# Seven groups of instructions change places in VectorE's queue, in batches 3 and 4

## The chip, the cores and the metric

The kernel runs on one core of a Trainium2 chip. The metric is the device time of one execution in microseconds. The kernel before took 396.45 us, the median of three runs (395.72 to 396.65).

## The reference

Two blocks follow each other. The first is an mLSTM cell over 4 batches, 8 heads, 768 steps and a head size of 40; the second is a Fourier mix with a two-layer perceptron on the 320 joined features.

```python
for t in range(S):                                    # mLSTM, per batch and head
    m_new = max(f[t] + m, i[t])
    C = exp(f[t] + m - m_new) * C + exp(i[t] - m_new) * outer(v[t], k[t])
    n = exp(f[t] + m - m_new) * n + exp(i[t] - m_new) * k[t]
    y[t] = sigmoid(o[t]) * (C @ q[t]) / max(abs(n @ q[t]), 1)
x = y as (batch, 768, 320)
u = x + real(fft(fft(x, axis=1), axis=2))             # Fourier mix
un = (u - mean(u)) / sqrt(var(u) + 1e-6)              # over the 320 features
out = u + maximum(un @ w_ch1, 0) @ w_ch2              # 320 -> 1280 -> 320
```

## The kernel before, in words

**Tiles and stages.** In the text the batches are 1 to 4; in the code b is 0 to 3. A batch has six chunks of 128 steps (c = 0 to 5). Of batches 2 to 4 each chunk goes through the mLSTM in halves of 64 steps; then the whole batch goes through the Fourier mix (two steps of matrix products), and then through the perceptron. The stages of neighbouring batches overlap: while the perceptron of one batch runs on TensorE, the mLSTM of the next runs in between, and after it the mix of the next.

**The steps that the change touches**, with the lines of the profile:

- `halves_weigh` (L672): VectorE multiplies a chunk's scores, in a bank of PSUM, by its weights W. `halves_from_chunk` (TensorE, L519) then multiplies W by the values.
- `mlstm_finish` (L712 to L720, five instructions): VectorE forms the denominator and multiplies the heads' result `ph`, in PSUM, by the gate. There is one bank pair for the heads: the next chunk's `halves_from_state` (TensorE, L519 `ph<-C,qg`) writes where `mlstm_finish` has read. The chunks 0, 1 and 3 are written into `so` and moved to their rows by DMAs (`halves_rows`, L728); chunks 2, 4 and 5 are written straight into `x`.
- `halves_add` (L667): VectorE adds a product from PSUM to the state C.
- `mix_add` (L957 to L963, six instructions): VectorE adds the result `pu` of the feature transform to `x` in four pieces and takes mean and variance. The chunks come in the order 0, 5, 1, 4, 2, 3; a pair shares one bank of `pu`. ScalarE's `mix_center` (L971) follows, then a transpose on TensorE (L978 `put`).
- `mlp_sums` (L1106, four instructions): the first layer is done by a scheme with seven products in place of eight, which needs sums of the inputs: T3, a new B12, T2 and T4, in this order.
- `mlp_block`: one pass of this scheme over two columns of hidden blocks, in four steps. VectorE adds products from PSUM (L1127) to the hidden values h; TensorE's products are L1118 and the short ones of the remaining 64 features L1123. A pass uses four banks; the next pass begins in the bank of the product p3, once VectorE has added it.
- `mlp_out_pair`: the second layer, also by seven products, two chunks at a time (three pairs n, four steps each). Two banks x and y alternate. After each product VectorE adds it, scaled, to the output (`residual`, L1187), which frees the bank for the next product (TensorE, L1237).
- `hidden_sums` (L1223): VectorE's sums for that scheme.

**What sets the order.** Nothing is scheduled by a compiler. `at(slot, phase, function, ...)` enters a call in a plan; at the end the plan is sorted by slot, then phase, and the calls issue their instructions in that order, each engine's queue being filled so. The phases are named EVAC 0, FILL 1, MAIN 2, FILL_PE 3. A step of the perceptron on TensorE is at MAIN of its slot, with the VectorE additions that belong to it. The perceptron of batch 2 fills the slots 63 to 94, that of batch 3 the slots 95 to 126, that of batch 4 those from 127 on. The mLSTM of batch 3 begins at slot 53 and its mix at slot 83; for batch 4 it is 83 and 115. Chunk c of a batch has its own slot s, three more for each c. An engine works its queue in this order and waits at a semaphore where an input is not there yet.

```python
            at(s + 1, FILL + 0.55 if b == 1 and c > 0 else MAIN + 0.7, halves_weigh, b, c)
            at(s + (5 if (b, c) == (2, 2) else 4), FILL + 0.3 if b == 1 else MAIN + 0.55, mlstm_finish, b, c)
            at(a, FILL if b < 2 else MAIN + 0.5, mix_add, b, c)
            at(s_mlp, EVAC + 0.5, mlp_sums)
```

Of the kernel before, what the change touches and what calls it, by code (L numbers as in the profile page):

```python
# [53 lines left out]
def kernel(  # L54
# [69 lines left out]
    def at(slot, phase, fn, *args):  # L124
        plan.setdefault((slot, phase), []).append((fn, args))
# [7 lines left out]
    EVAC, FILL, MAIN, FILL_PE = range(4)  # L133
# [628 lines left out]
    def plan_halves(b, s0, stride=3):  # L762
        for c in range(NT):
            s = s0 + stride * c
            t = 22 + 2 * c if b == 1 and c < 3 else s - 5
            at(t, FILL, mlstm_load, b, c)
            at(t, FILL, mlstm_load_max, b, c)
            at(34 if b == 1 and c == 2 else t + 1, FILL, mlstm_load_decay, b, c)
            at(s - 1, FILL, mlstm_load_o, b, c)
            at(s - 1, FILL, mlstm_scale_v, b, c)  # L770
            at(s - 1, FILL + 0.3, mlstm_exp, b, c, 0)
            at(s, FILL, mlstm_exp, b, c, NP)
            at(s, FILL_PE + 2.05, halves_scores, b, c)
            at(s, FILL_PE + 2.5, halves_to_state, b, c)
            for i in range(2):
                at(s + i, FILL + 0.05, halves_decay, b, c, i)
                at(s + 1 + i, FILL - 0.2, halves_add, b, c, i)
            at(s, FILL + 0.1, mlstm_scale_q, b, c)
            at(s + 1, FILL, mlstm_mask, b, c)
            at(s + 1, FILL + 0.55 if b == 1 and c > 0 else MAIN + 0.7, halves_weigh, b, c)  # L780
            end = c == NT - 1
            at(s + 3, MAIN - 0.1 if end else FILL_PE, halves_from_state, b, c)
            at(s + 3, MAIN - 0.1 if end else FILL_PE, halves_from_chunk, b, c, 0)
            at(s + 3, MAIN if end else FILL_PE + 0.5, halves_between, b, c)
            at(s + 3, FILL_PE + 3, halves_from_chunk, b, c, 1)
            at(s + 3, FILL_PE + 0.6, mlstm_tanh, b, c)
            at(s + (5 if (b, c) == (2, 2) else 4), FILL + 0.3 if b == 1 else MAIN + 0.55, mlstm_finish, b, c)
            at(s + 6, FILL - 0.6, halves_rows, b, c)


# [216 lines left out]
    def plan_mix(b, s0, x_done, s_feat, s_add, s_turn):  # L1007
        for j in range(TG):
            p = TG - 1 - j
            at(x_done[j] + (b > 1 and j == TG - 1), FILL + 0.5 if b < 2 else FILL_PE + 0.2, mix_fold, b, p)  # L1010
            if b == 0:
                at((s0 - 4, s0 - 2, s0)[j], FILL_PE + 4, mix_seq, b, p, (0, 1))
                at((s0 - 2, s0 - 2, s0)[j], FILL_PE + 4, mix_tail, b, p)
            elif b == 1 or j == 0:
                if b > 1:
                    for step, slot in enumerate((x_done[0], x_done[-1] + 2, x_done[-1] + 6)):
                        at(slot, FILL_PE + 0.25, mix_fold_again, b, step)
                at(s0, FILL_PE + 4, mix_seq, b, p, (0,))
                at(s0 + 1, FILL_PE + 4, mix_seq, b, p, (1,))
                at(s0 + 2, FILL_PE + 4, mix_tail, b, p)  # L1020
        for i in range(2):
            at(s0 + 1 if b == 0 else s0 + 1 + i, FILL, mix_seq_out, b, i)
        at(s0 + (1 if b == 0 else 3), FILL + 0.1, mix_tail_out, b)
        for p in range(TG):
            at(s_feat[p], FILL_PE + 4, mix_feat, b, p)
        for c, a, t in zip(ORDER, s_add, s_turn):
            at(a, FILL if b < 2 else MAIN + 0.5, mix_add, b, c)
            at(t, FILL + 0.1, mix_center, b, c)
            at(t, FILL_PE + (5 if b == 0 or c in ORDER[:4] else -0.1), mix_turn, b, c)
            if b > 0:  # L1030
                at(t, FILL_PE + 6, mix_turn_out, b, c)
            elif t < s_mlp:
                at(t + 1, FILL + 0.2, mix_turn_out, b, c)
            else:
                at(t + 1, EVAC, mix_turn_out, b, c)
# [62 lines left out]
    def mlp_u(gr, ch):  # L1098
        return uT_bufs[gr][:, ch].rearrange("p c t -> p (c t)")

    def mlp_sums():

        T2, T3, T4 = w1x["T"]
        B11, B12, B21, B22 = mlp_u(0, 0), mlp_u(1, 0), mlp_u(0, 2), mlp_u(1, 2)
        for out, x, y in ((T3, B22, B12), (B12, B12, B11), (T2, B22, B12), (T4, B21, T2)):
            nc.vector.tensor_tensor(out=out, in0=x, in1=y, op=OP.subtract)  # L1106

    def mlp_block(b, i, step):
# [200 lines left out]
    def plan_batch(b, s_mlstm, s_mix, s_mlp):  # L1309
        (plan_halves if b > 0 else plan_mlstm)(b, s_mlstm)  # L1310
        done = [s_mlstm + n for n in ((16, 19, 22) if b == 0 else (18, 21, 22))]
        assert s_mix >= done[-1] and s_mlp >= s_mix + 9
        late = [s_mlp + 2 * c for c in range(TG)]
        if b == 0:
            feat = [s_mix + 1, s_mix + 1, s_mlp + 3]
            turn = [s_mix + 2, s_mix + 3, s_mix + 4]
            add = turn + [s_mlp, s_mlp + 4, s_mlp + 5]
            late = [s_mlp + 2, s_mlp + 5, s_mlp + 7]
        else:
            feat = [s_mix + c for c in ((3, 4, 6) if b == 1 else (3, 4, 7))]  # L1320
            add = [s_mix + c for c in ((4, 4, 5, 6, 7, 7) if b == 1 else (4, 5, 5, 6, 8, 9))]
            turn = [s_mix + c for c in ((5, 6, 6) if b == 1 else (6, 7, 8))]
            late = [s_mix + c for c in ((7, 8, 8) if b == 1 else (9, 10, 10))]
            at(s_mlp, EVAC + 0.5, mlp_sums)
        plan_mix(b, s_mix, done, feat, add, turn + late)
        s = s_mlp + NFF + 2
        at(s, FILL + 0.6, mix_rstd, b)
        for n in range(3):
            at(s + 3 * n if b == 0 else s, FILL + 0.65, mix_rstd_step, b)
        plan_mlp(b, s_mlp)  # L1330

    s_mlp = 31
    plan_batch(0, 0, 22, s_mlp)
    plan_batch(1, 32, 54, s_mlp + MLP_SLOTS)
    plan_batch(2, 53, 83, s_mlp + 2 * MLP_SLOTS)
    plan_batch(3, 83, 115, s_mlp + 3 * MLP_SLOTS)
    for n in range(4):
# [149 lines left out]
```

## Time and profile before

| | us |
|---|---|
| median of three runs | 396.45 |
| the profiled execution | 395.51 |
| its span | 393.8 |
| TensorE busy (PE) | 378.9 (96%) |
| VectorE busy (DVE) | 277.9 (71%) |
| ScalarE busy (ACT) | 172.1 (44%) |
| GpSimd busy (POOL) | 134.3 (34%) |
| TensorE's granted clock over the span | 1.0 |

The span is the time from the first to the last instruction; 1.7 us of the execution lie outside it. A line of the timeline gives start, duration, engine, line, operation, the tile written and the tiles read, the shapes and a count where equal instructions were merged. Square brackets give the engine's idle time ahead of it and the instruction that ended the idle time. Consecutive VectorE instructions overlap by some 0.08 us, so a group's length is taken from start to start.

### The profile page before, as it was taken

The numbers are of one execution on the slowest core, as the hardware profiler recorded it, in microseconds if no ns is written. First come the engines' busy times: TensorE is split into PE (matmuls) and PEld (weight loads), VectorE is DVE, ScalarE is ACT, GpSimd is POOL, SyncE is SP. The second block draws the span as 40 slices with busy tenths as digits, with TensorE's granted clock in tenths as the row PEclk, the third lists the DMA queues.
The fourth block names the chain that finished last, engine by engine and source line by source line (L and its number), as shares of the span: only waits on it lengthen the run. The fifth ranks groups of instructions, "written<-read, shape, count | busy, mean of one in ns | idle before, by whom it ended". The sixth has DMA issues, their size and how long they took to land.

```text
span 393.8 us, 10580 instructions
## 1 busy us (share of the span) xinstructions
PE 378.9 (96%) x4174; PEld 276.4 (70%) x4174; DVE 277.9 (71%) x671; ACT 172.1 (44%) x481; POOL 134.3 (34%) x237
## 2 busy tenths in 40 slices
PE   8999899999999999998999989989999899999996
PEld 6877555556567677664579979755588896556996
DVE  8789987698698678566974598777655785336652
ACT  6987367377362214654452315454530123454000
POOL 5648515277946323281344133641500000020000
PEclk9999999999999999999999999999999999999999
DMA  7888499478593435529300636400000010000101
GB/s 223 301 238 244 138 242 262 168 227 224 161 232 97 138 88 169 152 82 228 98 16 31 157 83 195 123 20 2 0 2 33 0 36 33 2 0 0 35 33 35
DMA packets 25631, 44.78 MB, mean 114 GB/s; under 512 B 5727, under 2 KB 14766, under 8 KB 25454
## 3 DMA queue, kind: packets, MB, share of 16 engines
q1 hardware_dynamic: 25582, 44.11, 39.1%
q8 instruction: 33, 0.54, 0.6%
q14 instruction: 16, 0.13, 0.1%
HBM read 38.49 MB, written 4.12 MB: 108 GB/s over the span
## 4 chain that ended last, share of the span: by engine, by line
PE 74%; DVE 18%; issue 3%; ACT 3%; POOL 1%; DVEq 0%; ACTq 0%; POOLq 0%
PE po L1237 18%; PE pm L1118 15%; PE po L1181 8%; PE pm L1056 6%; PE ph L519 4%; PE pm L1123 4%; PE pu L935 3%; PE ps L519 3%; PE pm L1047 2%; PE put L978 2%; DVE h L1127 2%; PE pz L904 1%; PE pz L892 1%; DVE so L716 1%; DVE x L1187 1%
## 5 line engine op out<-in xcount | busy, mean ns | idle before, releaser
L1187 DVE SCALAR_TENSOR_TENSOR x<-po,rstd,x 128x160 f32<-128x160 f32 (+1 forms) x69 | 26.9, 394 | 41.5 <-PE po L1237 36.8
L1127 DVE TENSOR_TENSOR h<-h,pm 128x384 f32<-128x384 f32 x60 | 30.5, 549 | 29.0 <-PE pm L1123 13.8
L652 POOL TENSOR_TENSOR C<-C,decB 128x164 f32<-128x164 f32 x30 | 15.9, 530 | 70.1 <-DVE C L667 58.7
L1118 PE MATMUL pm<-uT,w_sb 128*128 128x384 f32 x90 | 37.7, 506 | 2.0 <-DVE h L1127 1.3
L491 ACT ACTIVATE W<-W,colT 128x64 f32<-128x64 f32 x144 | 37.5, 338 | 1.1 <-DMA W<-M_d 1.1
L1181 PE MATMUL po<-w_sb,h 128*128 128x320 f32 x120 | 34.3, 435 | 0.0
L515 POOL TENSOR_SCALAR_AFFINE_SELECT W<-W 64x512 f32<-64x512 f32 x36 | 27.3, 758 | 10.8 <-ACT W L491 9.3
L1002 POOL TENSOR_TENSOR t<-rstd 128x6 f32<-128x6 f32 x12 | 3.3, 273 | 80.7 <-DVE v L996 80.2
L1237 PE MATMUL po<-T,S 128*128 128x160 f32 x180 | 27.9, 302 | 1.5 <-DVE x L1187 1.5
L1056 PE MATMUL pm<-uT,w_sb 128*128 128x384 f32 x80 | 29.2, 500 | 0.1
L1181 PEld LDWEIGHTS po<-w_sb,h 128*128 128x128 f32 x120 | 22.3, 190 | 9.5 <-issue 0.6
L501 POOL TENSOR_TENSOR qg<-qk,Gb 128x512 f32<-128x512 f32 (+1 forms) x21 | 27.4, 1306 | 1.9 <-DMA qk<-in_qkT 1.3
L1237 PEld LDWEIGHTS po<-T,S 128*128 128x128 f32 x180 | 25.5, 190 | 3.2 <-DVE x L1187 2.0
L1118 PEld LDWEIGHTS pm<-uT,w_sb 128*128 128x128 f32 x90 | 15.5, 189 | 16.3 <-DVE h L1127 7.4
L1237 PE MATMUL po<-w_sb,h 128*128 128x160 f32 x180 | 26.3, 300 | 0.0
L1237 PEld LDWEIGHTS po<-w_sb,h 128*128 128x128 f32 x180 | 25.2, 190 | 1.4 <-DVE x L1187 0.3
L1174 ACT ACTIVATE h<-h 128x384 f32<-128x384 f32 x45 | 23.1, 520 | 2.0 <-DVE h L1127 2.0
L983 ACT COPY uT<-put 128x384 f32<-128x384 f32 x24 | 11.1, 477 | 29.0 <-PE put L978 29.0
L507 POOL TENSOR_TENSOR vw<-kvt,colT 128x328 f32<-128x328 f32 x23 | 19.3, 838 | 12.2 <-DMA qk<-in_qkT 10.1
L1123 PE MATMUL pm<-uT,w1t_sb 64*128 64x384 f32 x120 | 23.4, 508 | 0.0
L971 ACT ACTIVATE uc<-x 128x384 f32<-128x384 f32 x24 | 14.4, 613 | 17.9 <-DVE x L963 11.9
L1056 PEld LDWEIGHTS pm<-uT,w_sb 128*128 128x128 f32 x80 | 14.1, 189 | 9.6 <-issue 1.9
(241 smaller groups left out, 840.8 us busy)
## 6 DMA issues: line engine op xcount, KB each, us to landing
kvt<-in_kv SPq DMA_DIRECT2D x24, 336.0 KB
qk<-in_qkT SPq DMA_DIRECT2D x48, 160.0 KB
raw<-in_w SPq DMA_DIRECT2D x10, 640.0 KB
Gb<-G_d SPq DMA_DIRECT2D x36, 128.0 KB
W<-M_d SPq DMA_DIRECT2D x36, 128.0 KB
so<-in_o SPq DMA_DIRECT2D x24, 160.0 KB
out<-x SPq DMA_DIRECT2D x24, 160.0 KB
x<-so SPq DMA_DIRECT2D x9, 140.0 KB
```

What stands on the lines that cost most here:

```text
L491: nc.scalar.activation(out=k.W[:, h, :], in_=M, func=AF.Exp, scale=-1.0, bias=colT[:, c, 0, b * H + h:b * H + h + 1])
L501: nc.gpsimd.tensor_tensor(out=k.qg[:, :, t], in0=k.qk[:, 0, :, t], in1=k.Gb[:, :, t], op=OP.mult)
L515: nc.gpsimd.affine_select(out=W, in_=W, compare_op=OP.is_ge, fill=0.0, base=base, pattern=[[0, H], [step, LH]], channel_multiplier=-1)
L519: nc.tensor.matmul(out, w, x, start=start, stop=True, skip_group_check=True)
L1056: nc.tensor.matmul(k.pm[i], w1_sb[:, ch, f0:f0 + L], u[2 * ch], start=(ch == 0 and not ahead), stop=(ch == 1 and ahead), skip_group_check= ...
L1118: nc.tensor.matmul(bank, w, u, start=start, stop=True, skip_group_check=True)
L1123: nc.tensor.matmul(bank, block(w1t_sb, i)[rows], mlp_u(gr, 1)[rows], start=False, stop=True, skip_group_check=True)
L1127: nc.vector.tensor_tensor(out=h, in0=h, in1=bank, op=OP.add)
L1174: nc.scalar.activation(out=h, in_=h, func=AF.Relu, scale=-1.0)
L1181: nc.tensor.matmul(k.po[gr, i], hidden(gr, f)[:, i * L:(i + 1) * L], w2_sb[:, f, :], start=(f == 0), stop=(f == NFF - 1))
L1187: nc.vector.scalar_tensor_tensor(out=u, in0=po, scalar=k.rstd[:, c:c + 1], in1=u, op0=OP.mult, op1=OP.add)
L1237: nc.tensor.matmul(po, a[:, f], w[:, f], start=start and f == 0, stop=f == half - 1, skip_group_check=True)
```

## The change

Only VectorE's queue changes its order. The queues of TensorE, ScalarE, GpSimd and of the DMAs (SyncE) keep their instructions and their order; VectorE has the same instructions. By their places in VectorE's queue:

- **A**: `mlstm_finish` of batch 3, chunk 4 goes from behind to ahead of three additions L1127 of batch 2's perceptron (slot 69, from phase 2.55 to 1.3).
- **B**: `mix_add` of batch 3, chunk 0 goes from behind to ahead of two residuals L1187 (slot 87, from phase 2.5 to 1.7).
- **C**: `halves_weigh` of batch 4, chunk 2 goes behind one `halves_add` L667 and two residuals L1187 (from slot 90, phase 2.7 to slot 91, phase 2.1).
- **D**: `mlstm_finish` of batch 4, chunk 3 goes from behind the first L1127 of batch 3's perceptron to ahead of it and of one `halves_add` (slot 96, from phase 2.55 to 0.7). T4, the last of the four sums L1106, goes from ahead of these to behind that L1127 (from slot 95, phase 0.5 to slot 96, phase 2.6).
- **E**: `mix_add` of batch 4, chunk 0 goes ahead of two residuals L1187 (slot 119, from phase 2.5 to 1.7), and that of chunk 5 ahead of the two residuals after them (from slot 120, phase 2.5 to slot 119, phase 2.5).

```diff
-            at(s + 1, FILL + 0.55 if b == 1 and c > 0 else MAIN + 0.7, halves_weigh, b, c)
+            if (b, c) == (3, 2):
+                at(s + 2, MAIN + 0.1, halves_weigh, b, c)
+            else:
+                at(s + 1, FILL + 0.55 if b == 1 and c > 0 else MAIN + 0.7, halves_weigh, b, c)
...
-            at(s + (5 if (b, c) == (2, 2) else 4), FILL + 0.3 if b == 1 else MAIN + 0.55, mlstm_finish, b, c)
+            at(s + (5 if (b, c) == (2, 2) else 4), {(2, 4): FILL + 0.3, (3, 3): FILL - 0.3}.get((b, c), FILL + 0.3 if b == 1 else MAIN + 0.55), mlstm_finish, b, c)
...
-            at(a, FILL if b < 2 else MAIN + 0.5, mix_add, b, c)
+            at(a, FILL if b < 2 else MAIN - 0.3 if c == 0 else MAIN + 0.5, mix_add, b, c)
...
-    def mlp_sums():
+    def mlp_sums(n0, n1):
...
-        for out, x, y in ((T3, B22, B12), (B12, B12, B11), (T2, B22, B12), (T4, B21, T2)):
+        for out, x, y in ((T3, B22, B12), (B12, B12, B11), (T2, B22, B12), (T4, B21, T2))[n0:n1]:
...
-            add = [s_mix + c for c in ((4, 4, 5, 6, 7, 7) if b == 1 else (4, 5, 5, 6, 8, 9))]
+            add = [s_mix + c for c in ((4, 4, 5, 6, 7, 7), (4, 5, 5, 6, 8, 9), (4, 4, 5, 6, 8, 9))[b - 1]]
...
-            at(s_mlp, EVAC + 0.5, mlp_sums)
+            at(s_mlp, EVAC + 0.5, mlp_sums, 0, 3 if b == 2 else 4)
+            if b == 2:
+                at(s_mlp + 1, MAIN + 0.6, mlp_sums, 3, 4)
```

## The prediction

> **What bounds the kernel now.** I read the page first: PE is busy 378.9 of 393.8 us, at a granted clock of 1.0. So time can only come from PE's idle stretches or from PE's work, and the change leaves PE's queue as it is. The second view is PE's own timeline from 172 us on. After the start of batch 3's mLSTM it shows these stops above a tenth or two of a us, apart from one of 0.30 (175.69, on ScalarE) and two of 0.22 and 0.24 (194.61 and 330.88, on VectorE):
>
> ```profile
> 181.69 0.68 PE L519 MATMUL ph<-C,qg 40*64 40x41 f32 x32 [1.03 <-DVE x L720]
> ...
> 227.68 1.62 PE L1237 MATMUL po<-T,S 128*128 128x160 f32 x10 [1.08 <-DVE x L1187]
> ...
> 240.08 1.62 PE L1237 MATMUL po<-T,S 128*128 128x160 f32 x10 [0.45 <-DVE x L1187]
> ...
> 253.66 0.91 PE L1118 MATMUL pm<-uT,w_sb 128*128 128x384 f32 x2 [0.34 <-DVE uT L1106]
> ...
> 259.51 0.91 PE L1118 MATMUL pm<-uT,w_sb 128*128 128x384 f32 x2 [1.04 <-DVE h L1127]
> ...
> 314.36 1.63 PE L1237 MATMUL po<-T,h 128*128 128x160 f32 x10 [1.00 <-DVE x L1187]
> ```
>
> The bracket is the point: every one waits for VectorE, though VectorE is busy only 71% of the span. The third view, VectorE's timeline at the same places, tells whether it was late because it had too much to do or because it stood waiting at the wrong instruction. Near 181, 222, 256 and 306 us:
>
> ```profile
> 175.69 0.32 DVE L667 TENSOR_TENSOR C<-C,ps 128x164 f32<-128x164 f32 x1
> 178.50 1.48 DVE L1127 TENSOR_TENSOR h<-h,pm 128x384 f32<-128x384 f32 x3 [2.50 <-PE pm L1123]
> 179.90 0.16 DVE L712 TENSOR_SCALAR den<-ph 128x8 f32<-128x8 f32 x1
> ...
> 222.03 0.38 DVE L1187 SCALAR_TENSOR_TENSOR x<-po,rstd,x 128x160 f32<-128x160 f32 x1 [2.97 <-PE po L1237]
> 222.84 0.38 DVE L1187 SCALAR_TENSOR_TENSOR x<-po,rstd,x 128x160 f32<-128x160 f32 x1 [0.43 <-PE po L1237]
> 223.14 0.31 DVE L957 TENSOR_TENSOR x<-x,pu 128x161 f32<-128x161 f32 x1
> ...
> 256.04 0.55 DVE L1127 TENSOR_TENSOR h<-h,pm 128x384 f32<-128x384 f32 x1 [0.36 <-ACT h L1150]
> ...
> 305.74 0.38 DVE L1187 SCALAR_TENSOR_TENSOR x<-po,rstd,x 128x160 f32<-128x160 f32 x1 [1.14 <-PE po L1237]
> ```
>
> VectorE stands idle for 2.50 us, then 2.97 us, just before it is late: the work behind the waiting instruction was ready. The change pulls that work into these gaps.
>
> **What the Trainium skill says.** "PSUM — Partial Sum Buffer", section "Engine vs sequencer instructions", calls VectorE's queue a strict FIFO and says that matmuls start and complete in program order. The trace agrees: `mlstm_finish`, ready at 176.2, starts at 179.90, after the three L1127. "SBUF — State Buffer", section "Who interferes with whom", says that a VectorE instruction with two SBUF inputs contends with a GpSimd instruction that reads SBUF. The trace agrees: the four L1106 take 0.81, 1.52, 0.88 and 0.89 us at 251.24 to 255.4, where GpSimd works without a break (250.26 to 255.04), and 0.55 or 0.56 each at 329.7, where it does nothing. "TensorE: Matmul & The Clock Gate", section "What's actually happening", says that the clock is released by activity. No gap here cost clock (1.0 throughout), so filling gaps should change none.
>
> **A, the first normalising.** Its inputs: `ph` ends at 176.13, the gate's tanh at 176.01, VectorE is free at 176.01. Its length is 181.47 - 179.90 = 1.57 us, so it runs from about 176.2 to 177.8, ahead of 178.50, and delays nothing. The three additions stay at 178.50, the weighing L672 follows at 179.90 in place of 181.47. PE's preceding L1118 (179.86, 0.81) ends at about 180.66; `from_state` can start there, and its next products need the weighing at 181.17, which ends at 180.6. The whole 1.03 us goes. Later work here (VectorE's 185.45 waits 1.72 us for PE) follows PE; the row DMAs of chunk 3 were issued at 172.6 to 174.6, long before.
>
> **B, `mix_add` of chunk 0.** `pu` is complete at 219.39 + 0.70 = 220.09. Its length is 224.81 - 223.14 = 1.67 us: 220.15 to 221.85, inside the gap that ends at 222.03 (margin 0.2; beyond it still nothing happens until the product at 223.73 needs the bank). The two residuals keep their times; the normalising, weighing and L667 after them come 1.67 us earlier, and the residual on which PE waits, before at 227.25, can start at 227.25 - 1.67 = 225.58 and ends at 225.96. PE's previous product ends at 226.60. The 1.08 us go. VectorE itself comes out 0.91 us earlier (the second residual waits for PE: 226.64 in place of 227.55).
>
> **C, the weighing.** From 226 to 242 VectorE has no idle time, so at 240.08 it is late by load. PE now wants the residual 1.08 us earlier, VectorE is 0.91 earlier: the wait would be 0.45 + 0.17 = 0.62. The weighing (239.42 - 238.82 = 0.60) steps behind the residual. Left: 0.02; gain 0.43. The weighing is needed only by the products at 243.48, over 3 us later.
>
> **D, the second normalising and T4.** From 248.17 on VectorE is loaded; B12, at which PE waits 0.34 (253.66), stays where it is. The first addition in the next bank, L1127 at 258.91, holds up PE by 1.04. Ahead of it stand the same instructions in the new order, without the 0.36 idle of 256.04: `ph` is ready at 253.3, so the normalising starts at T2's end (254.56) and the copy on which L1127 waits (ACT, 256.0) is done when its turn comes (256.36). So at least 0.36; up to 0.33 more if T4 is free of GpSimd in its new place (0.56 in place of 0.89). But GpSimd's L652 and L507 move behind `halves_add` to about 256.4 to 257.8, over T4's new place: I take 0.40. What is behind the moved work: the L1127 must end before PE's short products enter its bank (second pair, about 257.1); it ends at 256.91, a margin of 0.2. T4 is wanted at 260.25, done at 257.7. A contended normalising would cost up to 0.9 (what B12 suffered, 1.52 - 0.56, about), so D lies between -0.5 and +0.7.
>
> **E, two `mix_add`.** `pu` is ready at 303.80, VectorE free at 304.53: chunk 0 runs to 306.2 and delays the residual of 305.74 by 0.5; PE needs its bank only at 307.44 (margin 0.8). Chunk 5 then runs in 306.9 to 308.6, before the residual of 309.00. After 310.66 only chunk 1 is left before the residual on which PE waits: 312.3 to 312.7 in place of 313.96. PE's transpose ends at about 313.36, so the 1.00 us goes. The last bank of `pu` is free at 314.4, PE wants it at 314.8.
>
> **Sum.** 1.03 + 1.08 + 0.43 + 0.40 + 1.00 = 3.94 us. Against the profiled execution: 395.51 - 3.94 = 391.6. The median of the runs is 0.94 above that execution, so I forecast 396.45 - 3.94 = 392.5. No DMA is moved in SyncE's queue; the rows of batch 4, chunk 3 are issued some 1.9 us sooner at 258.2, where SyncE was waiting for them.
>
> **Rivals.**
>
> *Part is given back.* After B, VectorE is loaded to 242 us and trails PE's gain by 0.17; if the 0.2 us margins are spent (semaphores, a contended instruction), C gives nothing and D at most 0.1, and one of the three large stops returns in half. 3.94 - 0.43 - 0.3 - 0.5 = 2.7: 393.7. For it: four margins are of 0.2 us or so. Against it: the three large ones rest on idle gaps of 2.5 and 3.0 us, or for E on 3.3 us of work moved out of the way.
>
> *No change.* The gaps close, but what comes later waits for something of its own pace: then 396 or so. For it: the next batch's loads and ScalarE's exponentials are not moved. Against it: in the list of waits from 172 to 270 us no row has ScalarE, GpSimd or VectorE waiting for a load; and from 262 to 314 PE has no stop at all.
>
> *Slower, by a late load.* PE comes 3 us earlier to batch 4's last chunk; if its W (issued 244.99 to 246.1, read by ScalarE at 255.91) met the row DMAs in the DMA queues, ScalarE would wait and then the weighing and PE, one for one. It bites only if W lands more than 255.91 - 246.1 = 9.8 us after its issue, and from 9.8 + 3.9 + 1.2, about 15 us, the kernel is slower by 1.2 us: 397.7. Against it: DMA is little used there, and W's issue waits for PE's reads and so shifts along.
>
> **How the numbers follow.** A measurement of this kernel can tell 0.3% (1.2 us) from no change. Full gain, 391.7 to 393.3: 0.66. Part given back, 393.3 to 395.2: 0.22. No change: 0.06. Slower: 0.06. The range 391.6 to 394.7 takes in D's upper end (0.3 more) and most of the second case. Faster 0.88, same 0.06, slower 0.06.
>
> **What would show it.** PE's stops at 181, 227 and 314 are gone, the one at 240 below 0.1, that at 259 near 0.6, the one at 253.66 still 0.3. VectorE's gap before the three L1127 shrinks from 2.50 to 0.7 us, the one before L1187 at 222 from 2.97 to 0.2 or so. The times of the stages shift by 1.0, 2.1, 2.5, 2.9 and 3.9 us. I am wrong if a stop of PE appears that was not there, above all on L1127's bank near 257 us or on ScalarE's exponentials after 250 us, or if `mlstm_finish` in its new place starts late because `ph` is.

## The result: 392.09 us, and the profile after

The kernel after takes 392.09 us, the median of four runs (391.26 to 392.19), against 396.19 for the kernel before beside it (395.72 to 396.65). The ratio is 0.9894, with a 95% interval of 0.9877 to 0.991. The difference is 4.10 us. The forecast was 392.5, made from the first three runs of before (median 396.45); taken from 396.19 it would have been 392.25.

The profiled execution of after took 392.19 us, with a span of 390.4 at a granted clock of 0.999. The first lines of its page and its chain:

```profile
PE 379.6 (97%) x4174; PEld 277.3 (71%) x4174; DVE 278.0 (71%) x671; ACT 172.1 (44%) x481; POOL 134.9 (35%) x237
...
PE 78%; DVE 14%; issue 3%; ACT 3%; POOL 1%; DVEq 0%; ACTq 0%; POOLq 0%
```

The busy time of VectorE is the same as before to 0.1 us (277.9, now 278.0). In the chain of work its share falls from 18 to 14%, and TensorE's rises from 74 to 78%. So no work was saved; it no longer stands in the way.

TensorE's own timeline of after, from 172 us on. These are all its stops of 0.2 us or more but two that were there before (194.53 with 0.21 and 327.52 with 0.24, on VectorE):

```profile
176.75 0.44 PE L519 MATMUL ph<-kvt,W 64*64 64x41 f32 x16 [0.30 <-ACT warm L699]
...
238.50 1.62 PE L1240 MATMUL po<-T,S 128*128 128x160 f32 x10 [0.30 <-DVE x L1190]
...
252.08 0.91 PE L1121 MATMUL pm<-uT,w_sb 128*128 128x384 f32 x2 [0.35 <-DVE uT L1109]
257.20 0.91 PE L1121 MATMUL pm<-uT,w_sb 128*128 128x384 f32 x2 [0.31 <-DVE h L1130]
```

The stops of 1.03, 1.08 and 1.00 us are gone, that of 1.04 is 0.31, that of 0.45 is 0.30, that of 0.34 is where it was. (Line numbers behind the first edit are three higher than before: the residual is L1190, the addition L1130, the sums L1109.)

VectorE's timeline of after at the places of A, B and D, E:

```profile
177.33 0.17 DVE L712 TENSOR_SCALAR den<-ph 128x8 f32<-128x8 f32 x1 [0.27 <-PE ph L519]
...
179.56 1.48 DVE L1130 TENSOR_TENSOR h<-h,pm 128x384 f32<-128x384 f32 x3 [0.51 <-PE pm L1126]
180.96 0.68 DVE L672 TENSOR_TENSOR W<-ps,W 128x512 f32<-128x512 f32 x1
...
220.03 0.32 DVE L960 TENSOR_TENSOR x<-x,pu 128x161 f32<-128x161 f32 x1 [1.07 <-PE pu L938]
...
221.94 0.38 DVE L1190 SCALAR_TENSOR_TENSOR x<-po,rstd,x 128x160 f32<-128x160 f32 x1
...
252.06 0.88 DVE L1109 TENSOR_TENSOR raw<-uT 128x384 f32<-128x384 f32 x1
252.87 0.15 DVE L712 TENSOR_SCALAR den<-ph 128x8 f32<-128x8 f32 x1
...
254.74 0.55 DVE L1130 TENSOR_TENSOR h<-h,pm 128x384 f32<-128x384 f32 x1
255.20 0.65 DVE L1109 TENSOR_TENSOR m<-uT,raw 128x384 f32<-128x384 f32 x1
...
256.60 1.47 DVE L1130 TENSOR_TENSOR h<-h,pm 128x384 f32<-128x384 f32 x3
...
304.06 0.84 DVE L1190 SCALAR_TENSOR_TENSOR x<-po,rstd,x 128x160 f32<-128x160 f32 x2
...
387.31 0.38 DVE L1190 SCALAR_TENSOR_TENSOR x<-po,rstd,x 128x160 f32<-128x160 f32 x1 [0.97 <-PE po L1240]
```

The wait of 2.50 us ahead of the three additions has become 0.27 and 0.51 with the normalising between them. Of the wait of 2.97 us ahead of the residual 1.07 are left, which now stand before `mix_add`; the residual itself waits for nothing. The first addition at 254.74 no longer waits for ScalarE (0.36 before), because the normalising has filled that time. At E the two residuals of 304.06 wait for nothing (1.14 and 0.43 before).

**A yardstick.** The two profiled executions differ by 395.51 - 392.19 = 3.32 us, the medians by 4.10. The reason lies in the first microseconds (see the last section): PE comes to the first row above, which is ahead of every moved instruction, at 175.69 in before and at 176.75 in after. So I measure each profile from that row to the start of the last residual. The two rows in before, from TensorE's and from VectorE's timeline:

```profile
175.69 0.44 PE L519 MATMUL ph<-kvt,W 64*64 64x41 f32 x16 [0.30 <-ACT warm L699]
...
390.66 0.38 DVE L1187 SCALAR_TENSOR_TENSOR x<-po,rstd,x 128x160 f32<-128x160 f32 x1 [0.97 <-PE po L1237]
```

before 390.66 - 175.69 = **214.97**, after 387.31 - 176.75 = **210.56**, a gain of **4.41 us**.

From mark to mark on PE, the part that each step gave, the late start taken out:

| mark on PE, before and after | shift | step | forecast | measured |
|---|---|---|---|---|
| heads' products 181.69, 181.65 | 1.10 | A | 1.03 | 1.10 |
| second-layer product 229.15, 227.71 | 2.50 | B | 1.08 | 1.35 |
| second-layer product 241.54, 239.96 | 2.64 | C | 0.43 | 0.14 |
| first-layer product 259.51, 257.20 | 3.37 | D | 0.40 | 0.73 |
| transpose 312.87, 310.75 | 3.18 | given back | none | -0.19 |
| feature transform 315.83, 312.44 | 4.45 | E | 1.00 | 1.27 |
| last residual 390.66, 387.31 | 4.41 | | 3.94 | 4.41 |

Where the shifts and the measured column do not add up, the rest is drift between the marks (0.05 from A to B, 0.04 behind E).

### The profile page after: what moved, and what is told of

Read it like the earlier page. It is cut to its first block, busy times and chain, and to the rows that moved or that the text cites. A ratio compares the mean times of both kernels' runs of the same rounds, so it can differ in the third digit from the quotient of the medians.

```text
span 390.4 us, 10585 instructions
## 1 busy us (share of the span) xinstructions
PE 379.6 (97%) x4174; PEld 277.3 (71%) x4174; DVE 278.0 (71%) x671; ACT 172.1 (44%) x481; POOL 134.9 (35%) x237
## 4 chain that ended last, share of the span: by engine, by line
PE 78%; DVE 14%; issue 3%; ACT 3%; POOL 1%; DVEq 0%; ACTq 0%; POOLq 0%
PE po L1240 20%; PE pm L1121 15%; PE po L1184 8%; PE pm L1059 7%; PE ph L519 4%; PE pm L1126 4%; PE pu L938 4%; PE ps L519 3%; PE pm L1050 2%; PE put L981 2%; PE pz L907 1%; PE pz L895 1%; DVE h L1130 1%; DVE so L716 1%; PE pM L221 1%
## 5 line engine op out<-in xcount | busy, mean ns | idle before, releaser
L1190 DVE SCALAR_TENSOR_TENSOR x<-po,rstd,x 128x160 f32<-128x160 f32 (+1 forms) x69 | 27.1, 394 | 37.4 <-PE po L1240 32.5
L1130 DVE TENSOR_TENSOR h<-h,pm 128x384 f32<-128x384 f32 x60 | 30.5, 548 | 27.1 <-PE pm L1121 12.6
L652 POOL TENSOR_TENSOR C<-C,decB 128x164 f32<-128x164 f32 x30 | 15.9, 531 | 67.5 <-DVE C L667 56.1
L515 POOL TENSOR_SCALAR_AFFINE_SELECT W<-W 64x512 f32<-64x512 f32 x36 | 27.3, 759 | 10.6 <-ACT W L491 9.1
L501 POOL TENSOR_TENSOR qg<-qk,Gb 128x512 f32<-128x512 f32 (+1 forms) x21 | 27.1, 1290 | 1.7 <-DMA qk<-in_qkT 1.6
L507 POOL TENSOR_TENSOR vw<-kvt,colT 128x328 f32<-128x328 f32 x23 | 19.7, 859 | 13.1 <-DMA qk<-in_qkT 10.1
```

The costliest lines, as they stand in the source:

```text
L501: nc.gpsimd.tensor_tensor(out=k.qg[:, :, t], in0=k.qk[:, 0, :, t], in1=k.Gb[:, :, t], op=OP.mult)
L515: nc.gpsimd.affine_select(out=W, in_=W, compare_op=OP.is_ge, fill=0.0, base=base, pattern=[[0, H], [step, LH]], channel_multiplier=-1)
L1130: nc.vector.tensor_tensor(out=h, in0=h, in1=bank, op=OP.add)
L1190: nc.vector.scalar_tensor_tensor(out=u, in0=po, scalar=k.rstd[:, c:c + 1], in1=u, op0=OP.mult, op1=OP.add)
```

## The experiments

One profiled execution tells the yardstick to a few hundredths: kernels whose edits lie elsewhere repeat stretches to within 0.05 us, with one exception of 0.13 (see A alone). The total time of a single run is of no use below 1 us, since the start scatters by that much. All single parts below were made on the kernel before.

### B alone

```diff
-            at(a, FILL if b < 2 else MAIN + 0.5, mix_add, b, c)
+            at(a, FILL if b < 2 else MAIN - 0.3 if c == 0 and b in (2,) else MAIN + 0.5, mix_add, b, c)
```

> Part B alone. A run's start varies by about 1 us, so the gain is read from PE's product near 175.7 us (the first stop on ScalarE after 172 us) to the span's end. My theory (VectorE is loaded from 223 to 242 us, so a stop taken away at 227 returns in part at 240): no stop at 227, the stop at 240 grows from 0.45 to about 0.8 to 0.9 us, gain about 0.9 us. Rival (each stop stands for itself): the stop at 240 stays at 0.45, gain 1.1 to 1.2 us.

The run took 395.64 us, the yardstick 214.05: a gain of 0.92. PE has no stop near 227 any more. TensorE's timeline of this kernel, its only stop between 224 and 243 us:

```profile
240.21 1.63 PE L1237 MATMUL po<-T,S 128*128 128x160 f32 x10 [0.89 <-DVE x L1187]
```

The next stop grew from 0.45 to 0.89. That is the working of the prediction with one size changed: PE gained 1.35 us at B, VectorE only 0.91, so the residual is later by 1.35 - 0.91 = 0.44 for PE, and 0.45 + 0.44 = 0.89. What B is worth alone, 0.92, is what it saves VectorE.

### C alone

```diff
-            at(s + 1, FILL + 0.55 if b == 1 and c > 0 else MAIN + 0.7, halves_weigh, b, c)
+            if (b, c) == (3, 2):
+                at(s + 2, MAIN + 0.1, halves_weigh, b, c)
+            else:
+                at(s + 1, FILL + 0.55 if b == 1 and c > 0 else MAIN + 0.7, halves_weigh, b, c)
```

> Part C alone. My theory (the weighing only has to leave the way of the residual, VectorE catches up at its idle time near 243 us): the stop at 240 is gone, the stop at 227 stays at 1.08, gain 0.45 to 0.5 us. Rival (VectorE's load bounds this stretch, so an instruction put later comes back later): a stop appears behind 240, at the next residual or at the products of the weighed W near 243, gain 0 to 0.1 us.

The run took 395.94 us, the yardstick 214.36: a gain of 0.61. TensorE's stop near 227 us:

```profile
228.70 1.63 PE L1240 MATMUL po<-T,S 128*128 128x160 f32 x10 [1.08 <-DVE x L1190]
```

The stop at 240 is gone, the one at 227 untouched. The later ones are those of before to 0.01 us (0.34, 1.04, 1.01 and 0.24), and none is new, so the weighing was not wanted earlier than its new place gives it. The gain is larger than the stop's bracket by 0.16. B alone and C alone add up to 1.53, and in the kernel after the two together give 1.49. On this stretch VectorE has no slack, and what counts is its own time: 0.91 and 0.60.

### The two halves of D, each alone

First the second normalising without T4:

```diff
-            at(s + (5 if (b, c) == (2, 2) else 4), FILL + 0.3 if b == 1 else MAIN + 0.55, mlstm_finish, b, c)
+            at(s + (5 if (b, c) == (2, 2) else 4), {(3, 3): FILL - 0.3}.get((b, c), FILL + 0.3 if b == 1 else MAIN + 0.55), mlstm_finish, b, c)
```

> Part D without T4's move: the normalising of batch 4, chunk 3 goes ahead of the first L1127, T4 stays fourth of the four sums. My theory (D lives on the 0.36 us in which VectorE stands waiting for ScalarE's copy): the stop at 259 falls from 1.04 to about 0.7, gain about 0.35 us. Rival (D lives on T4, which leaves GpSimd's busy stretch): gain at most 0.1 us.

The run took 396.5 us, the yardstick 215.07: a loss of 0.10. The theory's numbers were missed. The rival's number (a gain of at most 0.1) was met, but not its reason, as T4's move alone shows below. In the list of PE's stops the one at 259 is gone, but its time is still there. TensorE's timeline of this kernel:

```profile
257.76 2.48 PE L1123 MATMUL pm<-uT,w1t_sb 64*128 64x384 f32 x8
```

and VectorE's:

```profile
258.09 0.55 DVE L1127 TENSOR_TENSOR h<-h,pm 128x384 f32<-128x384 f32 x1
```

The eight short products take 2.48 us where they took 1.56. They go in pairs into four banks, and the second pair's bank is the one that this first L1127 must free. Taken one by one, the first pair and the second start together in before, at 256.90 and 256.91. With T4 and the normalising both ahead of it, L1127 starts 258.09 - 254.51 = 3.58 us after PE's first product of the pass, where it was 256.04 - 253.66 = 2.38 before, and ends at 4.13, some 0.9 us behind the 3.25 at which PE comes to that bank (256.91 - 253.66). That is nearly all of the 0.92 by which the group has grown. A wait inside a merged group of equal instructions gives no bracket. The three additions after it do come 0.38 us sooner by the same measure (259.38 - 254.51 = 4.87, before 5.25), as the prediction's 0.36 says, but PE has lost by then what it could have won; at 260.17 it is only 0.19 ahead of before, and at the heads' products of 265.79, where it stops for 0.22, it is 0.10 behind.

Then T4 without the normalising:

```diff
...
-            at(s_mlp, EVAC + 0.5, mlp_sums)
+            at(s_mlp, EVAC + 0.5, mlp_sums, 0, 3 if b == 2 else 4)
+            if b == 2:
+                at(s_mlp + 1, MAIN + 0.6, mlp_sums, 3, 4)
```

> Part D with T4's move alone: T4 goes behind the first L1127, the normalising stays. My theory: T4 gets shorter by 0.2 to 0.3 us, but VectorE then waits the longer for ScalarE's copy ahead of L1127, about 0.36 + 0.8 us; the stop at 259 falls from 1.04 to about 0.8, or stays. Rival (T4's place is what counts): the stop falls to about 0.4, gain 0.6 us or more.

The run took 396.98 us, the yardstick 215.41: a loss of 0.44, more than I had allowed for. VectorE's timeline of this kernel, then TensorE's:

```profile
257.06 0.56 DVE L1127 TENSOR_TENSOR h<-h,pm 128x384 f32<-128x384 f32 x1 [1.28 <-ACT h L1150]
...
259.09 0.55 DVE L1106 TENSOR_TENSOR m<-uT,raw 128x384 f32<-128x384 f32 x1
```

```profile
260.99 0.91 PE L1118 MATMUL pm<-uT,w_sb 128*128 128x384 f32 x2 [1.51 <-DVE h L1127]
```

T4 had covered most of VectorE's wait for ScalarE's copy. Moved away alone, it leaves 1.28 us of idle time, and is then added to the load behind it. It is 0.34 us shorter there (0.55, before 0.89), but that is not enough: the stop grows by 0.47. So the two moves of D are no sum of two gains. T4 makes room, so that the first addition is not late; the normalising fills the room. Alone they cost 0.10 and 0.44, together, in after, they gave 0.73 at 257 us.

### The two halves of E, each alone

First chunk 0 of batch 4, then chunk 5:

```diff
-            at(a, FILL if b < 2 else MAIN + 0.5, mix_add, b, c)
+            at(a, FILL if b < 2 else MAIN - 0.3 if c == 0 and b in (3,) else MAIN + 0.5, mix_add, b, c)
```

> Half of part E: the addition of batch 4, chunk 0 goes ahead of two residuals, that of chunk 5 stays. My theory: chunk 0 alone only moves VectorE's idle time; VectorE still waits for PE at the residual of 310.4 us with the additions of chunks 5 and 1 behind it, so the stop at 314 stays at 1.00 and the gain is 0. Rival (each half is worth half): the stop falls to about 0.5.

```diff
-            add = [s_mix + c for c in ((4, 4, 5, 6, 7, 7) if b == 1 else (4, 5, 5, 6, 8, 9))]
+            add = [s_mix + c for c in ((4, 4, 5, 6, 7, 7), (4, 5, 5, 6, 8, 9), (4, 4, 5, 6, 8, 9))[b - 1]]
```

> The other half of part E: the addition of batch 4, chunk 5 goes ahead of the two residuals after it, that of chunk 0 stays behind the two before. My theory: chunks 0 and 5 then run one after the other from 306.9 to 310.2 us, the residual due at 309.0 comes at 310.2, and PE stops by about 0.45 at 310.6 for its bank; the stop at 314 is gone or below 0.1; gain 0.5 to 0.6 us. Rival (chunk 5 alone carries E): no new stop, gain 1.0 us.

Chunk 0 alone took 396.32 us, with a yardstick of 214.98 and so no gain; chunk 5 alone 395.45 us, yardstick 214.26, a gain of 0.71. TensorE's timeline of the first:

```profile
315.15 1.62 PE L1237 MATMUL po<-T,h 128*128 128x160 f32 x10 [1.01 <-DVE x L1187]
```

and of the second:

```profile
311.21 1.63 PE L1237 MATMUL po<-T,S 128*128 128x160 f32 x10 [0.26 <-DVE x L1187]
```

With chunk 0 alone, chunk 5 still stands in the crowd after 310 us, and the stop stays as it was. With chunk 5 alone the stop at 314 goes, but both `mix_add` now stand together ahead of an earlier residual, and PE stops there for 0.26 (0.45 was expected, and a gain of 0.5 to 0.6). Chunk 0's move is worth nothing alone and 1.27 - 0.71 = 0.56 behind that of chunk 5.

### A alone

```diff
-            at(s + (5 if (b, c) == (2, 2) else 4), FILL + 0.3 if b == 1 else MAIN + 0.55, mlstm_finish, b, c)
+            at(s + (5 if (b, c) == (2, 2) else 4), {(2, 4): FILL + 0.3}.get((b, c), FILL + 0.3 if b == 1 else MAIN + 0.55), mlstm_finish, b, c)
```

> Part A alone. My theory: the stop at 181 is gone, every later stop stays as it was (1.08, 0.45, 0.34, 1.04, 1.00), gain about 1.1 us from PE's product near 176 us to the last residual: the bracket of 1.03 and up to 0.1 for the restart. Rival (later work has a pace of its own): the gain shrinks by 0.3 us or more before 227.

The run took 395.33 us, the yardstick 214.04: a gain of 0.93. At 194 us PE has gained 1.13 (194.61 - 175.69 = 18.92 before, 194.22 - 176.43 = 17.79 here), and every later bracket is the same to 0.03. So the stop gave what was expected, 1.1, but not all of it reached the end: between 259 and 265 us 0.13 are lost again, far behind the place where the rival looked for a loss.

From PE's first-layer product behind the stop of 1.04 (259.14) to the heads' products (264.60) it is 5.46 us, in before 264.84 - 259.51 = 5.33. In after this stretch has 262.69 - 257.20 = 5.49; in the kernels with B, C, T4's move or half of E alone it has 5.33 or 5.34. The heads' products at its end need the bank that the normalising of chunk 4 reads. In this kernel VectorE stands idle for 0.22 us inside that normalising, and in after it begins 0.22 us later behind the `halves_add` ahead of it (0.46 instead of 0.24). What VectorE waits for there I have not settled.

### How much of the load comes from GpSimd

Both B12's 1.52 us and T4's price in the prediction rest on VectorE and GpSimd getting in each other's way. Here GpSimd's scaling of q (L501) and mask (L515) of batch 4, chunk 4 were put behind its next L652, away from the sums:

```diff
-            at(s, FILL + 0.1, mlstm_scale_q, b, c)
-            at(s + 1, FILL, mlstm_mask, b, c)
+            late34 = (b, c) == (3, 4)
+            at(s + 1 if late34 else s, FILL + 0.1, mlstm_scale_q, b, c)
+            at(s + 1, FILL + 0.15 if late34 else FILL, mlstm_mask, b, c)
```

> The kernel before with two GpSimd instructions groups (the scaled queries L501 and the mask L515 of batch 4, chunk 4) behind the next decay L652, so behind VectorE's four sums L1106 of batch 3. My theory (two SBUF inputs against GpSimd's reads): the four L1106 take 0.55 to 0.6 us each in place of 0.81 to 1.52, the stop at 253.7 (0.34) goes; the weighing of that chunk then waits for the later mask, so the stop at 259 stays or grows. Rival (the sums are slow for another reason, ScalarE or a DMA in the same tiles): the four L1106 keep their 0.8 to 1.5 us.

The run took 396.11 us, the yardstick 214.49: a gain of 0.48. VectorE's timeline of this kernel, the four sums (before: 0.81, 1.52, 0.88, 0.89):

```profile
252.33 0.81 DVE L1107 TENSOR_TENSOR e<-uT 128x384 f32<-128x384 f32 x1
253.17 0.56 DVE L1107 TENSOR_TENSOR uT<-uT,uT 128x384 f32<-128x384 f32 x1
253.77 0.56 DVE L1107 TENSOR_TENSOR raw<-uT 128x384 f32<-128x384 f32 x1
254.36 0.56 DVE L1107 TENSOR_TENSOR m<-uT,raw 128x384 f32<-128x384 f32 x1
```

Nothing was changed on VectorE, and three of the four fall to 0.56. The first still runs beside an L652 of GpSimd. That agrees with the Trainium skill, "SBUF — State Buffer", section "Who interferes with whom": a VectorE instruction that reads two inputs from SBUF contends with a GpSimd instruction that reads SBUF. PE's stop at 253.7 goes. The time freed turns into a wait of VectorE for ScalarE's copy (1.33 us ahead of the first addition, 0.36 before), and the stop at 259 becomes 1.17, so only 0.48 are left of it.

### The change once more, and five moves beyond it

> The changed kernel itself, as the measure for the next. From PE's product near 176 us to the span's end 213.6 us, 4.4 to 4.5 us less than before; in time 4.0 to 4.5 us less than before.

The kernel after, a second time: 392.02 us (391.24 to 392.19, five runs), ratio 0.9884 (0.9868 to 0.99), yardstick 210.59. The gain by the yardstick is 4.38, the first time 4.41.

The next kernel does to the five stops that after still has what the change did to the others: the last sum of the hidden values of batch 2 one step later, the weighing of batch 4's chunk 4 behind the additions, T3 and B12 of batches 3 and 4 one step sooner, and a sum of weights from slot 75 to 78.

```diff
-            if (b, c) == (3, 2):
+            if (b, c) in ((3, 2), (3, 4)):
...
-                        at(s, MAIN + 0.6, hidden_sums, n + 1, (j,))
+                        at(*((s + 1, MAIN + 0.05) if (b, n, j) == (1, 1, 4) else (s, MAIN + 0.6)), hidden_sums, n + 1, (j,))
...
-            at(s_mlp, EVAC + 0.5, mlp_sums, 0, 3 if b == 2 else 4)
+            if b > 1:
+                at(s_mlp - 1, MAIN - 0.05, mlp_sums, 0, 2)
+            at(s_mlp, EVAC + 0.5, mlp_sums, 2 if b > 1 else 0, 3 if b == 2 else 4)
...
-        at((56, 57, 58, 75)[n], FILL + 0.4, out_weight_sums, n)
+        at((56, 57, 58, 78)[n], FILL + 0.4, out_weight_sums, n)
```

> The changed kernel with five more moves in VectorE's queue: one sum of the second layer's weights of batch 2 goes behind three L1127 near 194 us; S4 of the last pair of batch 2 goes behind two residuals near 238; T3 and B12 go ahead of the last residual of the batch before, for batches 3 and 4 (252 and 327 us); the weighing of batch 4, chunk 4 goes behind three L1127 near 257. My theory (what VectorE does ahead of the instruction for which PE waits is what counts, where it is not needed sooner): the five stops left after 190 us (0.21, 0.30, 0.35, 0.31, 0.24) go or fall below 0.1, gain over the changed kernel 1.0 to 1.5 us. Rival (VectorE is loaded there, what is moved behind makes a later instruction late): gain under 0.4 us, with new stops within a few us behind each.

390.46 us (390.05 to 390.88), ratio 0.9849 (0.9832 to 0.9866); yardstick 208.75. The gain over after by the yardstick is 1.8, more than the 1.0 to 1.5 expected. The same kernel a second time, because 1.5 us in time stand beside a scatter of 1:

> The kernel with five more moves, again, as the measure for the next: 208.7 us from PE's product near 176 us to the last residual, as before; time 390.0 to 390.9 us.

389.89 us (389.28 to 390.69), ratio 0.9844 (0.9824 to 0.9864); yardstick 208.77, a gain of 6.20 over before and again 1.8 over after. TensorE's share of the chain is 87%. Its timeline has no stop of 0.2 us from 172 us to the end but the one of 0.30 on ScalarE. One wait is left that shows no bracket:

```profile
252.97 2.02 PE L1126 MATMUL pm<-uT,w1t_sb 64*128 64x384 f32 x8
```

0.46 above the 1.56 of the other passes: the first addition is late there again. B12 took 0.70 us in its new place, but T2 1.34 and L716 0.95, beside the same work of GpSimd that has gone nowhere.

The last kernel goes after those 0.46 us. The second normalising and the weighing of chunk 4 stand between the first and the second of the three additions L1127, and their own entries in the plan go:

```diff
...
+            if (b, i) == (2, 0):
+                mlstm_finish(3, 3)
+                halves_weigh(3, 4)
```

> One move more: the second normalising of part D and the weighing after it go between the first and the second of the three L1127 that follow. In the kernel with five moves the short products L1123 still stop for about 0.46 us inside their group (2.02 in place of 1.56 us), for the first L1127, which stands behind that normalising. My theory: the group takes 1.56 us again and the normalising is done just when PE wants its bank; gain 0.2 to 0.5 us. Rival (VectorE is full between 249 and 258 us, the stop only moves): a stop of 0.3 us or more at the next products from the state or of the weighed W, gain 0 or a loss of up to 0.4 us.

390.64 us (389.36 to 390.73), ratio 0.9851 (0.9832 to 0.9871); yardstick 209.06, which is 0.29 worse, as the rival had it. The eight short products take 1.56 us again, and TensorE's timeline has two new stops:

```profile
257.40 0.68 PE L519 MATMUL ph<-C,qg 40*64 40x41 f32 x32 [0.42 <-DVE so L720]
...
261.65 0.68 PE L519 MATMUL ph<-C,qg 40*64 40x41 f32 x32 [0.21 <-DVE x L720]
```

VectorE idles 1.28 us for ScalarE's copy ahead of the first addition, since nothing fills that time any more, and then the normalising is late for PE. At this place every order tried leaves something late. By the yardstick the faster of these kernels is the one with the five moves; the times (389.28 to 390.88 in its two series, 389.36 to 390.73 here) do not tell the two apart.

## Why the prediction was right, and where its steps were off

The time (392.09 for 392.5) and the reading behind it held: PE waited for VectorE, and VectorE was late because it stood at an instruction whose input was not there. The working's sum is 0.47 too small by the yardstick (4.41 for 3.94). In the difference of medians, 4.10, that shows less, and as the start scatters by 1 us, a time within 0.4 us of the forecast is in part luck. The sum is helped by luck too: A, B, D and E were put too low by 0.07, 0.27, 0.33 and 0.27, C was put too high by 0.29, and 0.19 was given back that no step had.

**A, right.** 1.10 for 1.03. The normalising runs when `ph` is there, the additions wait 0.51 after it (forecast: the gap shrinks to 0.7), the weighing is in time. A alone gave 1.13 at 194 us, of which 0.93 were left at the end.

**B, the mechanism right, the stop priced too low.** The step took the loss to be the bracket, 1.08. It was 1.35, since this stop cost more than its idle time. TensorE's timeline in before and in after:

```profile
225.08 1.52 PE L1237 MATMUL po<-w_sb,S 128*128 128x160 f32 x10
...
229.15 1.52 PE L1237 MATMUL po<-w_sb,s_last 128*128 128x160 f32 x10
```

```profile
224.99 1.52 PE L1240 MATMUL po<-w_sb,S 128*128 128x160 f32 x10
226.35 1.52 PE L1240 MATMUL po<-T,S 128*128 128x160 f32 x10
227.71 1.52 PE L1240 MATMUL po<-w_sb,s_last 128*128 128x160 f32 x10
```

From the first to the last it is 4.07 us before and 2.72 after. Without a stop each group starts 1.36 us after the one ahead, though it takes 1.52: they overlap by 0.16. With a stop that overlap is lost, and the group after it takes 1.62. So 1.08 + 0.16 + 0.10 = 1.34.

**C, too high, for the same reason.** The forecast left 0.02 of the stop; 0.30 are left. PE came 1.35 sooner in place of 1.08, and VectorE's forecast of 0.91 + 0.60 was right: 0.45 + 1.35 - 0.91 - 0.60 = 0.29. B and C together were forecast at 1.51 and gave 1.49. What bounded the two was VectorE's time, and only the split between them was wrong.

**D, a gain as forecast but too low, and misread as to which half carries it.** "At least 0.36" from the idle time, with T4 as an extra, does not stand: the normalising alone lost 0.10. The margin of 0.2 for the first addition, which the step names, was not there: the second pair of short products was put at 257.1, but it starts with the first, at 256.91. With both moves the addition is in time by a hair (it starts 2.66 us after PE's first product and ends at 3.21, against 3.25 when its bank is wanted), and without T4's it is late by 0.9. VectorE's timeline of before, to set beside that of after above:

```profile
253.64 0.88 DVE L1106 TENSOR_TENSOR raw<-uT 128x384 f32<-128x384 f32 x1
254.56 0.89 DVE L1106 TENSOR_TENSOR m<-uT,raw 128x384 f32<-128x384 f32 x1
...
258.91 1.47 DVE L1127 TENSOR_TENSOR h<-h,pm 128x384 f32<-128x384 f32 x3
```

From T2's start to the three additions VectorE took 258.91 - 253.64 = 5.27 us before and 256.60 - 252.06 = 4.54 after: 0.73 less, of which 0.36 is the idle time, 0.24 T4 (0.57 from start to start in place of 0.81), and 0.13 overlap of neighbours. I had put T4 at nearly nothing, as GpSimd would be in its new place too; it took 0.65, hardly more than the 0.56 without GpSimd. The stop fell from 1.04 to 0.31 (forecast near 0.6). Behind it 0.16 came back at the heads' products of 262.69, which no step had looked at. It cannot be booked to D: A alone, with D's instructions where they were, loses 0.13 there.

**E, right.** 1.27 for 1.00, again bracket plus 0.27. The work that stood after 310.66 was the cause: with chunk 5 away from it the stop went, with chunk 0 alone it did not.

**What stayed.** The stop before the product that reads the new B12, "still 0.3", measured 0.35. **The rivals.** The change did what it says. Part was given back in two places (C left 0.30 of its stop where 0.02 was forecast, and 0.16 came back at 262.69), but no large stop came back, and B alone shows how it would have: 0.44 of 1.35 turned into the next stop. No load became late: no stop of PE or wait of VectorE shown here names one.

## What to carry to other kernels

When the bound engine stops and the engine it waits for is idle most of a gap just before, look at which instruction that engine stood at and what stood ready behind it; moving the ready work ahead was worth 4.4 us of 395 here, and five more moves of the same kind another 1.8. Price it by the queue that is late, not by the stop: where that engine is loaded from one stop to the next, only the time taken off its queue comes out (0.91 of B's 1.35), and where it must meet two deadlines, two moves that lose alone may win together. After each move look for a merged group that has grown (1.56 to 2.48), since a wait inside one shows no bracket.

## What was not expected of the hardware

**A stop of PE can cost more than its bracket.** Two stops in front of ten products 128 x 160 cost 0.27 us more than the idle time shown, 0.16 for the overlap with the group ahead and 0.10 for a longer first group. 1.35 for 1.08 at B, 1.27 for 1.00 at E. Ahead of the heads' products it was less: 1.10 for 1.03 at A.

**Which of two engines pays may turn on which began first.** T4 on VectorE (0.55 us where GpSimd does nothing) and L507 on GpSimd (0.74 in before) meet in after, in the kernel with five moves and in the last one. In both executions of the first two T4 begins 0.19 or 0.20 us ahead and takes 0.64 or 0.65, and L507 takes 1.05. In the last kernel L507 begins 0.24 us ahead and takes its 0.74, and T4 takes 0.91. No run was made to test this order.

**The start scatters by 1 us.** The first eight transposes of the kernel, near 4.6 us, the same instructions in all runs, take a different time in each execution, and the row at 176 us moves with it, to within 0.4 us. TensorE's timeline of before and of after:

```profile
4.59 1.05 PE L221 MATMUL pM<-w_sb,ident 128*128 128x128 f32 x8
```

```profile
4.75 1.91 PE L221 MATMUL pM<-w_sb,ident 128*128 128x128 f32 x8
```

| execution | full clock on record from | the eight transposes | row at 176 |
|---|---|---|---|
| before | 4.42 | 1.05 | 175.69 |
| five more moves, second time | 4.57 | 1.05 | 175.78 |
| chunk 5 alone | 5.13 | 1.24 | 176.34 |
| A alone | 5.78 | 1.55 | 176.43 |
| after, second time | 6.29 | 1.79 | 176.57 |
| after | 7.08 | 1.91 | 176.75 |
| five more moves | 7.17 | 1.92 | 176.86 |

All edits lie behind 172 us in time, and the kernels with five moves stand near both ends of the table. The Trainium skill, "TensorE: Matmul & The Clock Gate", section "What's actually happening", says that the array starts throttled and is released by an activity window that runs free of the kernel's start, so that the release falls differently in each run. The traces agree. Beside the instructions a trace keeps records of TensorE's granted clock (second column). The first begins at 4.42 to 7.43 us in the 13 of 14 traces that have any. The later it begins, the longer the transposes take, until it begins behind their end, from where on they stay at 1.91 or 1.92. In all 13 that record lasts 382.29, 385.71 or 389.12 us, lengths in steps of 3.41. For the time ahead of it the page's mean counts full clock, so a mean of 1.0 does not speak of the first microseconds. No run here set when the clock is released, so that part is the skill's; that the start is also what spreads the times without a profile (before: 395.72 to 396.65) is a reading. It makes two single profiles a poor measure of 1 us.
